# Feed-forward passes of 768 and 1024 tokens with sums kept in PSUM banks, in a fused attention and two-layer feed-forward kernel

## The chip, the cores and the metric

The kernel runs on one core of one Trainium2 chip. The metric is the device time of one execution in microseconds (us); lower is better. The engines are named as in the profile: PE is TensorE (matrix products; PEld is its weight load), DVE is VectorE, ACT is ScalarE, POOL is GpSimd, and SP is the engine whose queue issues nearly all DMA transfers.

## The reference

```python
def _attn_ref(q, k, v, cap):            # 4 batches, 12 heads, 448 tokens, 64 wide
    scores = np.matmul(q, k.transpose(0, 1, 3, 2)) / np.sqrt(q.shape[-1])
    scores = cap * np.tanh(scores / cap)
    attn = np.exp(scores - np.max(scores, axis=-1, keepdims=True))
    attn = attn / (np.sum(attn, axis=-1, keepdims=True) + 1e-09)
    return np.matmul(attn, v)
x = attention, as 1792 tokens x 768
h = x @ w_in;   x = (h - np.tanh(h)) @ w_out               # 768 -> 2048 -> 768
h = x @ w_in2;  out = (h / (1 + np.exp(-1.702 * h))) @ w_out2
```

The four weight matrices arrive as 64-bit floats. All of the feed-forward products are made from two parts of each operand, a high and a low one, so a product of two tiles is three matmuls: high by high, high by low, low by high.

## The kernel before

**Passes.** Attention runs first over 24 pairs of heads (four batches of six). The feed-forward then takes the 1792 tokens in two passes of 896 (two batches each). Each pass has four stages: `gemm_in(0)` (768 to 2048, then h - tanh h, made by `g_cubic` as a chain over ACT and DVE), the way out (2048 to 768), the second way in with its gate, and the rows stage `gemm_rows_seven` (2048 to 768, output rows). The trace's first pass spends 200.1 to 661.4 us in them, the second 661.4 to the end.

**Plain and seven-product stages.** `gemm_in(0)` of both passes, and the way out and the second way in of the first pass (`gemm_out`, `gemm_in(1)`), are plain: every weight chunk against all 896 tokens, in two column spans of 512 and 384 (`SPANS`). The second pass's `gemm_out_seven` and `gemm_in_seven` and both row stages split each operand into 2x2 blocks and make seven block products instead of eight. Operand sums are made on DVE, of the weights ahead of time (`sums_a`, `sums_i`, `sums_b`, through DRAM) and of the activations in the stage (`right`, `left`). Product sums are added on DVE after each product. In the first two of these stages a block is 448 tokens. In the row stage the tokens are the stationary operand in tiles of 128, of which 896 holds seven: six go through the seven products, three to a half, and the seventh by plain products (`rest_products`, with its own split `rest_g`) that need four further weight chunks in each pass.

**Weights.** In the first pass each 64-bit chunk is fetched by DMA (`dbl_dma`, 768 KB, tiles `wd`), converted by ACT and DVE (`conv_exp` L168, `conv_low` L175, `conv_shift` L181, `conv_or` L185 into `wr`) and stored for later (`single`, 384 KB). `conv_or` ends with the store and with the fetch of the chunk three places ahead, whose buffer it has freed. If the chunk is used now, it is split (`wh` on ACT, `wl` on DVE L88). Sixteen chunks of the last matrix are converted beside others (`beside`): twelve in the way out, four in the second way in. So the way out carries 28 conversions and the second way in 20, less what is done early. Chunks are made ready two ahead of use (`LEAD`), in three `wh` buffers.

**Order.** DVE, ACT and SP each run one fixed list, written by the program's order and a scheduler when the kernel is built; a wait in it holds all that stands behind. `late` holds work that is issued some matmuls into the next product. Rows of `left(..)` for the next product stand behind the matmuls that last read the ring of split operands.

Of the kernel before, what the change touches and what calls it, by code (L numbers as in the profile page):

```python
# [37 lines left out]
def attention_moe_moe(ctx, tc, q, k, v, cap, w_in1, w_out1, w_in2, w_out2, out):  # L38
# [60 lines left out]
    xd = [[dr_p.tile([P, S], F32, name=f"xd{b}_{i}") for i in range(KM)] for b in range(B)]  # L99
    wrow = [dr_p.tile([4, NP // 2, S], F32, name=f"wrow{b}") for b in range(B)]  # L100
# [121 lines left out]
    SEVEN_B = ("11", "21", "22", "t2", "t3", "t1", "t4")  # L222
# [9 lines left out]
    for p, m in enumerate(SEVEN_B):  # L232
        rows_stream += [(t, WC, HW) for t in side_b[m]]
        if 2 <= p < 2 + KQ:
            rows_stream.append((side_b["12"][p - 2], WC, HW))
# [125 lines left out]
    def sums_b():  # L361
        for n in range(KH):
            j, a = n // 2, slice(n % 2 * HW, (n % 2 + 1) * HW)
            r = {m: s2[n % 2 * 4 + x][:, :HW] for x, m in enumerate(("11", "21", "12", "22"))}
# [21 lines left out]
    tt, tl, sc_t, ts_t, r_t, sum_t, xs = {}, {}, {}, {}, {}, {}, {}  # L386

# [122 lines left out]
    def pair_out(g):  # L510
        x = xs[g] = xs_p.tile([P, S], F32, tag="xs", name="xs")
        hi_dve(x, r_t.pop(g)[:, :S])
        if g >= NB * NP:
            b, i = divmod(g, NP)
            nc.sync.dma_start(out=xd[b][i], in_=xs.pop(g))
# [7 lines left out]
    def batch_recip(b, half):  # L523
        a = slice(half * S // 2, (half + 1) * S // 2)
        w = w_t[b]
        ins = pin(nc.vector.reciprocal(out=w[:, a], in_=w[:, a]))
        if half:
            for n in range(4):
                nc.sync.dma_start(out=wrow[b][n], in_=w[n * SR:n * SR + NP // 2])
        return ins  # L530

    def w_rows(t, b, i):
        for j in range(2):
            nc.sync.dma_start(out=t[j * D:(j + 1) * D], in_=wrow[b][i % 2 * 2 + j, i // 2].partition_broadcast(D))

    def x_split(s, i, x):
        a = slice(s * S, (s + 1) * S)
        hi_act(xh[i][:, a], x)
        lo_dve(xl[i][:, a], x, xh[i][:, a])
# [4 lines left out]
    def attention():  # L544
# [5 lines left out]
        def x_part(n):  # L550
            s_, i = divmod(n, NP)
            return i, slice(s_ * S, (s_ + 1) * S)
# [21 lines left out]
        for g in range(NG):  # L574
# [3 lines left out]
            for n in x_of(g):  # L578
                pin(nc.vector.tensor_tensor(out=xs[n], in0=xs[n], in1=wb.pop(n), op=ALU.mult))
                i, a = x_part(n)  # L580
                hi_pool(xh[i][:, a], xs[n])
# [15 lines left out]
            for n in x_of(g):  # L597
                i, a = x_part(n)
                lo_pool(xl[i][:, a], xs.pop(n), xh[i][:, a])
# [14 lines left out]
            for n in x_of(g + 1):  # L614
                wb[n] = wb_p.tile([P, S], F32, tag="wb", name="wb")
                w_rows(wb[n], *divmod(n, NP))
# [30 lines left out]
    def swap_pools(**kinds):  # L647
        if "stack" in some:
            some.pop("stack").close()
# [26 lines left out]
    def g_cubic(a, f, ps):  # L676
# [6 lines left out]
        def rest():  # L683
# [19 lines left out]
            if plain[0] and f < KH and a.stop == NT:  # L703
# [7 lines left out]
        if f == KF - 1 and a.stop == NT and not plain[0]:  # L711
            late.append(lambda: list(splits.pop(0)))

    def g_gate(a, f, ps):
# [3 lines left out]
        if plain[0]:  # L718
            g = gr[f][:, a]
            nc.vector.scalar_tensor_tensor(out=g, in0=t, scalar=1.0, in1=ps, op0=ALU.add, op1=ALU.mult)  # L720
            if a.start == 0 and f < KH:
                late.append(lambda: left("11", f))
            if a.stop == NT:
                late.append(lambda: split(rest_g[f], gr[f][:, REST]))
# [6 lines left out]
    TH = 3 * P  # L731
    REST = slice(2 * TH, NT)
    gr, s2, ring, rest_g, last_t = [], [], [], [], []

    def open_plain():
        g_stack.close()
        p = pool("g_plain", 1)
        gr.extend(p.tile([P, NT], F32, name=f"gr{i}") for i in range(KF))
        s2.extend(p.tile([P, S], F32, name=f"gs{i}") for i in range(KH))
        ring.extend([p.tile([P, S], F32R, name=f"r{m}{i}") for m in "hl"] for i in range(KH))  # L740
        rest_g.extend([p.tile([P, P], F32R, name=f"rest{m}{i}") for m in "hl"] for i in range(KF))
# [5 lines left out]

    def right(p, k):
        g11, g12, g21, g22 = (gr[f][:, t * S:(t + 1) * S] for f in (k, KH + k) for t in range(2))
        if p == 1:  # L750
            x = s2[k]
            nc.vector.tensor_tensor(out=x, in0=g22, in1=g12, op=ALU.subtract)
            nc.vector.tensor_tensor(out=x, in0=x, in1=g11, op=ALU.add)
        elif p == 3:
            x = g12
            nc.vector.tensor_tensor(out=g11, in0=g12, in1=g11, op=ALU.subtract)
            nc.vector.tensor_tensor(out=x, in0=g22, in1=x, op=ALU.subtract)
        elif p == 6:
            x = s2[k]
            nc.vector.tensor_tensor(out=x, in0=g21, in1=x, op=ALU.subtract)  # L760
        else:
            x = {0: g11, 2: g21, 4: g11, 5: g22}[p]
        split(ring[k], x)

    def left(name, k):
        g11, g21, g12, g22 = (gr[f][:, t * TH:(t + 1) * TH] for f in (k, KH + k) for t in range(2))
        x = {"11": g11, "21": g12, "22": g12, "t2": s2[k][:, :TH], "t3": g11, "t1": g21, "t4": g22}[name]
        if name == "22":
            s = s2[k][:, :TH]
            add(s, g21, ALU.add, g22)  # L770
            add(s, s, ALU.subtract, g11)
            add(x, x, ALU.subtract, s)
        elif name == "t3":
            add(x, x, ALU.subtract, g21)
        elif name == "t1":
            add(x, x, ALU.add, g22)
        split([t[:, :TH] for t in ring[k]], x)

    def gemm_in(layer):
        for f in range(KF):  # L780
            i, (wh, wl) = w_next()
            for a0, a1 in SPANS:
# [400 lines left out]
```

## Time and profile before

| what | value |
|---|---|
| three runs | 1093.85, 1097.28, 1097.44 us (median 1097.28) |
| profiled execution | 1094.2 us from its first to its last instruction; no other time is given for it |
| PE busy | 1081.3 us (99%), 5579 matmuls |
| DVE busy | 929.8 us (85%) |
| ACT busy | 668.7 us (61%) |
| DMA | 220.58 MB, mean 202 GB/s |
| PE clock granted | 0.9 or more of full speed in all 40 slices |

Busy time of PE is the union of rows whose ends are modelled, and neighbouring matmuls overlap in it; what a matmul costs in a stream is read from the distance of two starts. The kernel has stages with different limits, so the shares of the whole say little about one of them.

### The profile page before, as it was taken

Reading aid. Unit: us, or ns where it says so; the run is one execution under the profiler, and the core shown is the slowest. Engines: PE = TensorE matmul, PEld = TensorE weight load, DVE = VectorE, ACT = ScalarE, POOL = GpSimd, SP = SyncE. Lnnn points to the kernel's source line nnn. Section 1 sums busy time; section 2 is a strip of 40 time slices with the busy share of each in tenths; the row PEclk is TensorE's granted clock in tenths of the full one; section 3 lists DMA queues with packets and bytes.
Section 4 is the critical chain, followed back from the end, with each engine's and each line's share of the span. In section 5 each row is a group of like instructions: output and inputs, shape, how many; then the busy total and the mean of one; then the engine's idle time right before and its main releaser. Section 6 shows DMA issues by size and latency. Waiting matters only on the chain.

```text
span 1094.2 us, 16108 instructions
## 1 busy us (share of the span) xinstructions
PE 1081.3 (99%) x5579; PEld 887.0 (81%) x5579; DVE 929.8 (85%) x1467; ACT 668.7 (61%) x1022; POOL 59.1 (5%) x56
## 2 busy tenths in 40 slices
PE   9999998999999999999999999999999999999998
PEld 3333333688998888899899998889999999999998
DVE  4688999799997787889897885999999898889775
ACT  6898888799893433445245654767645554455453
POOL 0013443200000000000000000000000000000000
PEclk9999999999999999999999999999999999999999
DMA  6767786465537989889835768888555333333344
GB/s 142 206 187 199 192 234 192 148 209 173 188 116 265 318 305 332 292 287 313 285 110 170 227 201 276 313 287 291 183 192 176 107 123 102 102 110 107 119 144 142
DMA packets 156466, 220.58 MB, mean 202 GB/s; under 512 B 58672, under 2 KB 108640, under 8 KB 156384
## 3 DMA queue, kind: packets, MB, share of 16 engines
q1 hardware_dynamic: 155088, 218.94, 62.9%
q8 instruction: 44, 0.72, 0.3%
q10 hardware_dynamic: 1296, 0.61, 0.2%
q14 instruction: 38, 0.31, 0.1%
HBM read 160.83 MB, written 58.68 MB: 201 GB/s over the span
## 4 chain that ended last, share of the span: by engine, by line
PE 85%; DMA 6%; DVE 5%; ACT 2%; issue 2%; SPq 1%; ACTq 0%; DVEq 0%
PE ps_h L791 32%; PE ps_o L1018 15%; PE ps_h L938 10%; PE ps_y L854 10%; PE ps_pv L498 7%; PE ps_sc L457 5%; DMA wd<-in_moe_w_out_dram 4%; PE ps_o L997 3%; DVE wr L185 1%; DVE wd L175 1%; PE ps_qk L436 1%; PE ps_r L505 1%; PE ps_tl L467 1%; PE ps_y L816 1%; ACT wr L168 1%
## 5 line engine op out<-in xcount | busy, mean ns | idle before, releaser
L791 PE MATMUL ps_h<-xh,wh 128*128 128x384 f32 (+1 forms) x576 | 184.5, 365 | 0.3 <-ACT xh L76 0.3
L791 PE MATMUL ps_h<-xl,wh 128*128 128x384 f32 (+1 forms) x576 | 183.8, 364 | 0.0
L791 PE MATMUL ps_h<-xh,wl 128*128 128x384 f32 (+1 forms) x576 | 131.4, 362 | 0.1
L76 ACT CAST rh<-gr 128x384 fp32r<-128x384 f32 (+1 forms) x141 | 73.7, 528 | 82.8 <-PE ps_o L1018 36.4
L791 PEld LDWEIGHTS ps_h<-xh,wh 128*128 128x128 f32 x576 | 107.1, 188 | 13.8 <-ACT xh L76 1.0
L791 PEld LDWEIGHTS ps_h<-xl,wh 128*128 128x128 f32 x576 | 107.0, 188 | 11.9
L76 ACT CAST wh<-whole 128x768 fp32r<-128x768 f32 (+1 forms) x105 | 84.9, 810 | 50.4 <-PE ps_h L938 30.9
L791 PEld LDWEIGHTS ps_h<-xh,wl 128*128 128x128 f32 x576 | 104.6, 188 | 13.4 <-issue 1.4
L1018 PE MATMUL ps_o<-wl,rh 128*128 128x384 f32 x336 | 112.4, 335 | 1.1 <-DVE wl L88 1.1
L1018 PE MATMUL ps_o<-wh,rh 128*128 128x384 f32 x336 | 112.3, 334 | 0.0
L1018 PE MATMUL ps_o<-wh,rl 128*128 128x384 f32 x336 | 112.3, 334 | 0.0
L88 DVE TENSOR_TENSOR wl<-whole,wh 128x768 fp32r<-128x768 f32 (+1 forms) x105 | 96.5, 921 | 9.4 <-ACT wh L76 7.8
L168 ACT ACTIVATE wr<-wd 128x768 f32<-128x768 f32 x64 | 57.9, 909 | 69.6 <-DMA wd<-in_moe_w_out_dram 41.2
L88 DVE TENSOR_TENSOR rl<-gr,rh 128x384 fp32r<-128x384 f32 (+1 forms) x141 | 79.8, 573 | 13.7 <-ACT rh L76 12.9
L476 ACT ACTIVATE t<-ps_sc,tsc 128x896 f32<-128x896 f32 x72 | 70.0, 1008 | 26.6 <-PE ps_sc L457 26.6
L175 DVE TENSOR_SCALAR wd<-wd 128x768 uint16<-128x768 uint16 x57 | 59.5, 1044 | 24.9 <-ACT wr L168 24.7
L478 ACT ACTIVATE t<-t,cpos 128x896 f32<-128x896 f32 x72 | 72.5, 1044 | 0.4
L816 PE MATMUL ps_y<-gh,wh 128*128 128x512 f32 (+1 forms) x192 | 70.0, 365 | 1.6 <-DVE xl L88 1.4
L816 PE MATMUL ps_y<-gl,wh 128*128 128x512 f32 (+1 forms) x192 | 69.9, 364 | 0.0
L457 PE MATMUL ps_sc<-qk 64*128 64x448 f32 x288 | 68.2, 572 | 0.8 <-ACT qk L76 0.6
L498 PE MATMUL ps_pv<-t,rv 128*64 128x448 f32 x288 | 64.2, 551 | 3.9 <-ACT t L476 3.4
L1018 PEld LDWEIGHTS ps_o<-wl,rh 128*128 128x128 f32 x336 | 63.1, 188 | 1.6 <-DVE wl L88 1.4
(145 smaller groups left out, 2307.6 us busy)
## 6 DMA issues: line engine op xcount, KB each, us to landing
wd<-in_moe_w_in_dram SPq DMA_DIRECT2D x64, 384.0 KB
wd<-in_moe_w_out_dram SPq DMA_DIRECT2D x32, 768.0 KB
single<-wr SPq DMA_DIRECT2D x48, 384.0 KB
whole<-single SPq DMA_DIRECT2D x43, 384.0 KB
pair<-single SPq DMA_DIRECT2D x40, 384.0 KB
s<-pair SPq DMA_DIRECT2D x32, 384.0 KB
whole<-s SPq DMA_DIRECT2D x32, 384.0 KB
wh<-kept SPq DMA_DIRECT2D x25, 384.0 KB
```

Of the source, the lines that this page charges most:

```text
L76: pin(nc.scalar.copy(out=dst, in_=src))
L88: pin(nc.vector.tensor_tensor(out=dst, in0=src, in1=hi.bitcast(F32), op=ALU.subtract))
L175: pin(nc.vector.tensor_scalar(out=half[:, :, 2], in0=half[:, :, 1], scalar1=F64_LOW, scalar2=None, op0=ALU.mult))
L457: pin(nc.tensor.matmul(ps[:, j, :S], qk[a, kc], qk[a, :S], start=True, stop=True))
L476: pin(nc.scalar.activation(out=t, in_=ps[:, :, :S], func=AF.Tanh, scale=tsc))
L478: ins = pin(nc.scalar.activation(out=tt[g, c], in_=tt[g, c], func=AF.Exp, scale=cpos))
L498: pin(nc.tensor.matmul(ps[a, :S], w, t[:, j], start=(c == 0), stop=(c == KC - 1)))
L791: pin(nc.tensor.matmul(ps, w[:, kk, :], x[kk][:, a], start=(m == 0), stop=(m == len(seq) - 1)))
L816: nc.tensor.matmul(bank[e][:, :a1 - a0], w[:, kk, c], x[2 * j + kk][:, a0:a1], start=(j == 0 and m == 0), stop=(j == KF // 2 - 1 and m == ...
L854: nc.tensor.matmul(ps[e], w[:, kk, c], x, start=(k == 0 and m == 0), stop=(k == KH - 1 and m == 2))
L938: nc.tensor.matmul(ps, w, x, start=(m == 0), stop=(m == len(seq) - 1))
L1018: nc.tensor.matmul(ps[n], x[:, t], w[:, kk, :], start=(k == 0 and m == 0), stop=(k == KH - 1 and m == 2),)
```

## The change

The token passes become 768 and 1024. Both spans of a plain stage are then equal: 384 and 384 columns in the first pass, 512 and 512 in the second. The halves of the seven-product stages are 384 tokens (rows of pass one) and 512 (all of pass two), so no tile of tokens is left over; `rest_products`, `rest_g` and the four further weight chunks of each pass go away. Batch 1 of the attention output is cut at token 320: its first part is scaled and split during attention as before, the other 128 columns go through DRAM (`parts_of`, `xd`) with batches 2 and 3.

In the seven-product stages the products run in another order, and a later product adds onto the PSUM bank of an earlier one (`head`: for example s3 and 22 onto s2's bank in `gemm_in_seven`). The earlier value is read from the bank between the two. DVE's adds after products go from 7 to 5 for each of the eight steps of `gemm_in_seven`. The activation sums are made in place, four for each `k` of the eight instead of five, and the tiles `s2` are gone.

Two buffers change. The third `wr` buffer is held only through the way out of pass one (`open_plain` closes it); before, it stayed through the second way in too. `sums_b` works in two tiles `more` in the place of `s2`.

```diff
-    NB = 2
-    NPASS = B // NB
+    TOKENS = (6 * P, B * S - 6 * P)
+    FIRST = (0, TOKENS[0])
+    CUT = TOKENS[0] - S
...
-    NT = NB * S
-    SPANS = [(0, 512), (512, NT)]
-    TC = max(z - a for a, z in SPANS)
+    NT = max(TOKENS)
+    SPANS = [[(0, n // 2), (n // 2, n)] for n in TOKENS]
+    HT = NT // 2
+    TC = HT
...
-    SEVEN_B = ("11", "21", "22", "t2", "t3", "t1", "t4")
+    SEVEN_B = ("11", "t2", "21", "t3", "t1", "t4", "22")
...
     def open_plain():
         g_stack.close()
+        some.pop("wr")
+        some.pop("last").close()
         p = pool("g_plain", 1)
         gr.extend(p.tile([P, NT], F32, name=f"gr{i}") for i in range(KF))
...
+    def left(p, k):
+        th = TOKENS[now[0]] // 2
+        g11, g21, g12, g22 = (gr[f][:, t * th:(t + 1) * th] for f in (k, KH + k) for t in range(2))
+        if p == 1:
+            add(g21, g21, ALU.add, g22)
+            sub(g11, g21, g11)
+        elif p == 3:
+            sub(g11, g22, g11)
+        split([t[:, :th] for t in ring[k]], {0: g11, 1: g11, 2: g12, 3: g11, 4: g21, 5: g22, 6: g12}[p])
+        if p == 2:
+            sub(g12, g12, g11)
...
+            for name in ("11", "s2", "s1", "s3", "12", "s4", "22"):
...
+                head = {"12": "11", "s4": "s1", "s3": "s2", "22": "s2"}.get(name, name)
+                if name == head:
+                    banks[head] = ps_next("ps_h")
+                ps = banks[head]
...
+                elif name == "s2":
+                    u2 = temp("q")
+                    add(u2, ps, ALU.add, p1)
+                elif name == "s3":
+                    u3 = temp("t")
+                    add(u3, ps, ALU.add, p1)
+                    add(u3, banks["s1"], ALU.add, u3)
+                    gate(KH + j, HI, u3)
```

Two places on DVE matter below. The first is the end of `gemm_in(0)` of pass one. There `g_far`, `g_t`, `g_q` and `gl` are the steps of h - tanh h of one half of a chunk (the last two chunks here), and `wd`, `wr` and `wl` are the conversion of weight chunks of the next stage. Before:

```order
L698 COPY_PREDICATED g_q<-g_m,g_far 128x512
L88 TENSOR_TENSOR wl<-wr,wh 128x768
L695 TENSOR_TENSOR g_t<-g_v,g_t 128x384
L88 TENSOR_TENSOR gl_2114<-g_q,gh_2098 128x512
L697 SCALAR_TENSOR_TENSOR g_q<-g_q,g_t 128x384
L181 TENSOR_SCALAR wr<-wr 128x768
L698 COPY_PREDICATED g_q<-g_m,g_far 128x384
L185 SCALAR_TENSOR_TENSOR wr<-wd,wr 128x768
L88 TENSOR_TENSOR gl_2114<-g_q,gh_2098 128x384
L175 TENSOR_SCALAR wd<-wd 128x768
L181 TENSOR_SCALAR wr<-wr 128x768
L185 SCALAR_TENSOR_TENSOR wr<-wd,wr 128x768
```

And in the changed kernel:

```order
L183 TENSOR_SCALAR wr<-wr 128x768
L711 TENSOR_TENSOR g_t<-g_v,g_t 128x384
L187 SCALAR_TENSOR_TENSOR wr<-wd,wr 128x768
L90 TENSOR_TENSOR gl_2104<-g_q,gh_2088 128x384
L713 SCALAR_TENSOR_TENSOR g_q<-g_q,g_t 128x384
L177 TENSOR_SCALAR wd<-wd 128x768
L90 TENSOR_TENSOR wl<-wr,wh 128x768
L714 COPY_PREDICATED g_q<-g_m,g_far 128x384
L183 TENSOR_SCALAR wr<-wr 128x768
L187 SCALAR_TENSOR_TENSOR wr<-wd,wr 128x768
L90 TENSOR_TENSOR gl_2104<-g_q,gh_2088 128x384
L177 TENSOR_SCALAR wd<-wd 128x768
```

The steps of h - tanh h all work on 384 columns now, and two conversion steps `wr<-wd,wr` stand ahead of the last `gl` where before one did, the next having stood behind it.

The second place is one step of `gemm_in_seven` in pass two, where `part<-ps_h,part` reads a product's bank, `gr<-gr,..` is the end of a gate, and `gs` is an early operand sum of the row stage. Before:

```order
L907 SCALAR_TENSOR_TENSOR gr_4261<-gr_4261,part 128x448
L88 TENSOR_TENSOR wl<-whole,wh 128x384
L907 SCALAR_TENSOR_TENSOR gr_4254<-gr_4254,part 128x448
L313 TENSOR_TENSOR part<-ps_h,part 128x448
L313 TENSOR_TENSOR gs_4269<-gr_4253,gr_4261 128x384
L313 TENSOR_TENSOR gs_4269<-gs_4269,gr_4253 128x384
L313 TENSOR_TENSOR part<-ps_h,part 128x448
L88 TENSOR_TENSOR wl<-whole,wh 128x768
```

And in the changed kernel, where the second of the three reads here is that of s3's bank and the third that of s1's:

```order
L313 TENSOR_TENSOR part<-ps_h,part 128x512
L921 SCALAR_TENSOR_TENSOR gr_4251<-gr_4251,part 128x512
L313 TENSOR_TENSOR part<-ps_h,part 128x512
L90 TENSOR_TENSOR wl<-whole,wh 128x384
L313 TENSOR_TENSOR part<-ps_h,part 128x512
L90 TENSOR_TENSOR wl<-whole,wh 128x768
L921 SCALAR_TENSOR_TENSOR gr_4252<-gr_4252,part 128x512
L921 SCALAR_TENSOR_TENSOR gr_4244<-gr_4244,ps_h 128x512
```

A weight split stands between the read of s3 and the read of s1, and s1's bank is the one that s4 adds onto one product later.

## Rows read from the trace of the kernel before

**Rows 1.** Busy time by stage: length, engines (instructions), clock, DMA share, GB/s.

```profile
200.10:320.20 120.10, 120.10 (x598) 105.21 (x597) 110.09 (x183) 109.27 (x177) 0.00 (x0) 1.00 0.50 169
320.20:438.70 118.50, 116.93 (x577) 104.18 (x577) 94.54 (x128) 47.90 (x66) 0.00 (x0) 1.00 0.86 295
438.70:555.90 117.20, 116.93 (x578) 104.41 (x578) 100.96 (x173) 48.35 (x88) 0.00 (x0) 1.00 0.83 276
555.90:661.40 105.50, 104.40 (x602) 103.96 (x601) 86.99 (x151) 56.37 (x101) 0.00 (x0) 1.00 0.62 188
661.40:778.10 116.70, 116.61 (x578) 104.35 (x577) 104.63 (x181) 79.16 (x135) 0.00 (x0) 1.00 0.84 292
778.10:882.20 104.10, 104.10 (x505) 94.56 (x505) 98.95 (x168) 55.85 (x99) 0.00 (x0) 1.00 0.46 148
882.20:986.40 104.20, 104.20 (x506) 94.65 (x505) 89.85 (x159) 54.69 (x98) 0.00 (x0) 1.00 0.37 111
986.40:1094.30 107.90, 104.00 (x600) 103.67 (x599) 80.37 (x139) 51.96 (x88) 0.00 (x0) 1.00 0.43 129
```

**Rows 2.** Chain that ended last, in order of time: start, length, what.

```profile
207.81 112.57 PE ps_h L791 x559
...
332.46 5.48 DMA wd<-in_moe_w_out_dram
...
437.65 0.96 DVE wl L88
...
555.94 3.12 PE ps_o L1018 x18
```

**Rows 3.** TensorE timeline, one chunk of the second pass: start, length, instruction.

```profile
690.71 0.39 PE L791 MATMUL ps_h<-xh,wh 128*128 128x512 f32 x1
...
693.47 1.52 PE L791 MATMUL ps_h<-xh,wl 128*128 128x512 f32 x6
...
694.83 0.33 PE L791 MATMUL ps_h<-xh,wh 128*128 128x384 f32 x1
```

**Rows 4.** VectorE groups by shape, first layer of pass one: count, busy, mean ns.

```profile
L698 DVE COPY_PREDICATED g_q<-g_m,g_far 128x512 f32<-128x512 uint16 x15 | 11.2, 745 | 0.3
...
L697 DVE SCALAR_TENSOR_TENSOR g_q<-g_q,g_t 128x512 f32<-128x512 f32 x15 | 10.3, 687 | 1.2 <-ACT g_q L693 0.7
...
L698 DVE COPY_PREDICATED g_q<-g_m,g_far 128x384 f32<-128x384 uint16 x14 | 8.4, 601 | 0.1
...
L697 DVE SCALAR_TENSOR_TENSOR g_q<-g_q,g_t 128x384 f32<-128x384 f32 x14 | 7.9, 563 | 0.3
```

**Rows 5.** Busy time around the second stage, columns as in group 1.

```profile
326.00:332.00 6.00, 6.00 (x31) 5.26 (x30) 6.00 (x12) 2.86 (x6) 0.00 (x0) 1.00 0.01 4
...
338.00:350.00 12.00, 12.00 (x63) 10.96 (x62) 8.03 (x10) 4.07 (x5) 0.00 (x0) 1.00 0.97 351
...
338.00:440.00 102.00, 100.22 (x495) 89.03 (x493) 79.89 (x103) 39.34 (x51) 0.00 (x0) 1.00 0.93 321
```

**Rows 6.** VectorE timeline, the last activation half and the next conversion.

```profile
331.89 0.55 DVE L88 TENSOR_TENSOR gl<-g_q,gh 128x384 fp32r<-128x384 f32 x1
...
333.99 0.96 DVE L185 SCALAR_TENSOR_TENSOR wr<-wd,wr 128x768 uint32<-128x768 uint32 x1
```

**Rows 7.** Conversion step L185, two stretches: count, durations, first and last start.

```profile
L185 DVE SCALAR_TENSOR_TENSOR wr<-wd,wr x28: 936/958/961, 334.0 to 436.8; 128x768 uint32<-128x768 uint32 x28
...
L185 DVE SCALAR_TENSOR_TENSOR wr<-wd,wr x16: 948/959/975, 441.5 to 530.2; 128x768 uint32<-128x768 uint32 x16
```

**Rows 8.** Who waited for whom in the second stage: us, times, longest.

```profile
ACT wr L168 <- DMA wd<-in_moe_w_out_dram: 34.0, 15, 4.3
```

**Rows 9.** VectorE groups by shape, row stage of pass one.

```profile
L88 DVE TENSOR_TENSOR rl<-gr,rh 128x384 fp32r<-128x384 f32 x40 | 21.6, 550 | 1.5 <-ACT rh L76 1.4
...
L88 DVE TENSOR_TENSOR wl<-whole,wh 128x768 fp32r<-128x768 f32 x21 | 19.8, 950 | 2.1 <-ACT wh L76 2.1
```

**Rows 10.** Who waited for whom, ACT, second way in: us, times, longest.

```profile
ACT wr L168 <- DVE wl L88: 4.4, 7, 1.0
```

More of the change, by code (lines that the diff above doesn't have):

```diff
@@ L647, in swap_pools @@
     def swap_pools(**kinds):
-        if "stack" in some:
-            some.pop("stack").close()
+        for name in ("last", "stack"):
+            if name in some:
+                some.pop(name).close()
         some.clear()
@@ L710, in g_cubic @@
         late.append(rest_behind)
-        if f == KF - 1 and a.stop == NT and not plain[0]:
+        if f == KF - 1 and a.start and not plain[0]:
             late.append(lambda: list(splits.pop(0)))
@@ L971, in gemm_rows_seven @@
[L971 to L973 removed]
+            got, banks = {}, {}
+            p1 = u2 = u3 = None
+            for name in ("11", "s2", "s1", "s3", "12", "s4", "22"):
+                c, n = chunk_of[name], half_of.get(name, 0)
+                if j == 0:
+                    c, n = {"12": 3}.get(name, c), {"12": 0, "22": 1}.get(name, n)
+                first = c not in got
+                if first:
+                    got[c] = w_next()
+                i, (wh, wl) = got[c]
+                head = {"12": "11", "s4": "s1", "s3": "s2", "22": "s2"}.get(name, name)
+                if name == head:
+                    banks[head] = ps_next("ps_h")
+                ps = banks[head]
+                seq = [
+                    (w[:, 3 * n + kk, :], x[:, :HT]) for kk, (h, l) in enumerate(right_of[name])
+                    for w, x in ((wh, h), (wh, l), (wl, h))
+                ]
+                for m, (w, x) in enumerate(seq):
+                    nc.tensor.matmul(
+                        ps, w, x, start=(name == head and m == 0),
+                        stop=(m == len(seq) - 1), skip_group_check=True,
+                    )
+                    if m == 0 and first:
+                        ahead(i)
+                    if m == 3:
+                        run_late()
+                if name == "11":
+                    p1 = temp("far")
+                    nc.scalar.copy(out=p1, in_=ps)
+                elif name == "s2":
[6 more added lines that the diff above has]
+                    gate(KH + j, HI, u3)
+                elif name == "12":
+                    gate(j, LO, ps)
+                elif name == "s4":
+                    add(u2, ps, ALU.add, u2)
+                    gate(j, HI, u2)
+                elif name == "22":
+                    add(p1, ps, ALU.add, p1)
+                    gate(KH + j, LO, p1)
+                if j == KH - 1 and name in ("12", "s4", "22"):
+                    a = {"12": 0, "s4": 3, "22": 6}[name]
+                    late.extend(lambda k=k: left(0, k) for k in range(a, min(a + 3, KH)))
@@ L983, in gemm_rows_seven @@
-        third.append(sums[3])
-        rest = [ps_s.tile([P, 512], F32, tag="s", name="ps_o")[:, :HW] for _ in range(2)]
-        todo = [divmod(n, KM) for n in range(2 * KM)] if b0 + NB < B else []
+        room = [t[:, a:a + HW] for t in (*four_of_pairs(), more[0]) for a in range(0, t.shape[1], HW)]
+        p1, u2, u3 = (room[m * nt:(m + 1) * nt] for m in range(3))
+        third.append(more[1][:, :WC])
+        todo = [divmod(n, KM) for n in range(2 * KM)] if another else []
         loaded = []
@@ L992, in add_to @@
             nc.vector.scalar_tensor_tensor(out=dst, in0=ps, scalar=0.5, in1=x, op0=ALU.mult, op1=ALU.add)
-        def rest_products(k, f, half, wh, wl, first, last):
-            gh_f, gl_f = rest_g[f]
-            for m, (x, w) in enumerate(((gh_f, wh), (gh_f, wl), (gl_f, wh))):
-                nc.tensor.matmul(
-                    rest[half], x, w, start=(first and k == 0 and m == 0), stop=(last and k == KH - 1 and m == 2)
-                )
-        last = []
-        for p, name in enumerate(SEVEN_B):
-            ps = three()
-            end = p == 6 and b0 + NB == B
+        last, of = [], {}
+        if side:
+            until("b")
+        for p, name in enumerate(SEVEN_B):
+            head = {"21": "11", "t3": "t2", "t4": "t2", "22": "t1"}.get(name, name)
+            if name == head:
+                of[head] = banks()
+            ps = of[head]
+            end = p == 6 and not another
             for j in range(KQ):
@@ L1012, in gemm_rows_seven @@
                 last.clear()
-                order = [(n, *k) for n in range(3) for k in ks] if end else [(n, *k) for k in ks for n in range(3)]
+                order = [(n, *k) for n in range(nt) for k in ks] if end else [(n, *k) for k in ks for n in range(nt)]
                 for n, k, kk, u, v in order:
```

323 lines of the change are left out of this document (127 added, 196 removed).

## The prediction

> **What bounds the kernel now.** I read the stages first, then the chain, then the starts of matmuls, and last what DVE, ACT and the DMA do where the chain leaves PE. By stage [rows 1] PE is busy nearly throughout, but its cover differs: in the first layer of pass one DVE has 110.1 of 120.1 us; in the way out and the second way in the DMA share is 0.86 and 0.83; in pass two DVE is high (99.0 of 104.1 on the way out) and the DMA has room. The chain [rows 2] says the same. It runs along PE through the first layer (559 matmuls in 112.57 us), leaves PE early in the way out, goes through weight transfers and conversion steps from 332.46 to a weight split at 437.65 us, and runs along PE again, with 18 row matmuls in 3.12 us. So in the way out conversions arrive barely in time, and everywhere else matmuls set the time.
>
> A conversion there waits for its transfer: ACT's first step waited 34.0 us in 15 waits for weights [rows 8]. From 338 to 440 us the DMA engines are 0.93 busy at 321 GB/s; their best stretch has 0.97 and 351 [rows 5]. The reader is to see that this stage has two bounds within a few per cent of each other, and that only one of them depends on the number of tokens: weights are the same for 768 tokens as for 896.
>
> **What matmuls alone give.** By the distance of starts a 512-column matmul costs (694.83 - 690.71) / 18 = 228.9 ns, the last six of a span 226.7 [rows 3]. The first layer's mean is 112.57 / 559 = 201.4 ns, so its 384-column ones cost 173.9; in the rows they cost 3.12 / 18 = 173.3 [rows 2].
>
> Pass one: the first layer saves 559 x (201.4 - 173.9) ns = 15.4 us; the two further plain stages of 576 matmuls take 100.2 us each instead of 118.5 and 117.2 [rows 1], which saves 18.3 and 17.0; the rows have 504 matmuls for 600, 87.4 us instead of 105.5, which saves 18.1. Together -68.8. Pass two: 576 x 228.9 = 131.8 us instead of 116.7 (+15.1); twice 504 x 228.9 = 115.4 instead of 104.1 and 104.2 (+22.5); the rows 672 x 173.3 = 116.5 instead of 104.0 (+12.5). Together +50.1. So PE alone would be 18.7 us shorter. The tail behind the last matmul (107.9 - 104.0 = 3.9 us) stays.
>
> No trace here shows a stage of 512 columns only; I take 228.9, with 226.7 as the lower bound: 1584 x 2.2 ns = 3.5 us. The Trainium skill ("TensorE: Matmul & The Clock Gate", Back-to-back issue gap) gives N / 2.4 + 2.5 ns for an isolated gap, about 216 ns at 512 columns. By it the second pass would be some 20 us shorter than in my sum; the rows at 512, and those at 384 (173.3 against some 162), stand above the rule.
>
> **What the conversions take back.** The first layer of pass one leaves DVE behind. Its last activation step ends at 332.4 us, 12 us after PE has left the stage, and the next conversion step starts at 334.0 [rows 6]; from 326 to 332 the DMA stands still [rows 5], since the fetches stand behind these steps. In the change DVE's five steps per half are done on 384 columns instead of 512 in one half of two: 745 - 601 = 144 ns for the dearest, 687 - 563 = 124 for the cheapest [rows 4]. Five of these are 0.62 to 0.72 us a chunk, 16 chunks about 10.6 us. A conversion step that stood behind the last step now stands ahead of it (first place in the order shown), some 1.5 us more. So conversions resume 12 us earlier, not the 15.4 that PE gains.
>
> From there the work is unchanged: 28 conversions from 334.0 to 436.8, 3.81 us apart, and 16 more from 441.5 to 530.2 [rows 7]. None waits for more tokens, so a faster PE pulls none forward. At 12 us earlier the last is done at 519; the DMA may close ranks in the second way in, where its share is lower, and I take 4 us for that. Then come the last chunk's split and 36 matmuls of 173.9 ns: 515 + 2.5 + 6.3 = 524 us. PE alone would be there at 555.9 - 15.4 - 18.3 - 17.0 = 505. **The term is +19 us.** Bounds: at 351 GB/s throughout, the 195 us from 332 to 527 at about 321 become 178, and the stage ends near 510 (+5); with a shift of 9 us and no closing up it ends at 531 (+26). I take 524, since the shares of 0.93 leave little to close. The Trainium skill ("DMA: Bandwidth & Descriptors", Where 436 GB/s comes from) puts the HBM side at about 358 GB/s for one core; the best stretch's 351 agrees. By 358 throughout the stage would end near 507; this page speaks against a gain beyond that.
>
> The third `wr` buffer is missing in the second way in. With three, ACT waited 4.4 us for a split to free one [rows 10]. With two, this may double (4.4) or hide in the transfers (0); I take 2.
>
> **The rows of pass one.** DVE is busy 87.0 of 105.5 us [rows 1]. Ring splits (0.550 us) and weight splits (0.950) [rows 9] become few less: 28 weight chunks instead of 32, 15 bank reads instead of 24, the scaling of x 14% more. That leaves about 81 us under 87.4 of PE, 92% where it was 83%. The stage lost 1.5 us then; I add 2.6 now, with 0 and 8 as bounds.
>
> **Shared banks in pass two.** In `gemm_in_seven` a product is 9 matmuls, 2.06 us. Between s3's end and s4's first matmul DVE must read s3's bank, make a weight split and read s1's bank (second place in the order): 0.687 [rows 4] + 0.950 + 0.687 = 2.3 us. Eight steps lose 0.27 us each, 2.2 us; I take 2. Below, nothing, where the split is the half one; above, if each split also waits for its copy on ACT about as long as it lasts itself, 8 x 1.2 = 10. On the way out each bank has two thirds of a short round, 12 matmuls or 2.7 us, before it is written again, and DVE has less to do per matmul than before: nothing.
>
> Costed at nothing: the additional small transfers of batch 1 during attention (DMA off its path there), the operand sums of the rows, four for five (DVE, inside the 92%), `gemm_in(0)` of pass two, whose DMA share of 0.84 now has 15 us more room.
>
> **Sum.** -18.7 + 19 + 2 + 2.6 + 2 = +6.9 us on the profiled 1094.2, so 1101.1. That execution is 3.1 us under the median of the runs; the same step on 1097.3 gives **1104**.
>
> **Rivals.**
> (A) As above, 1104, from 1094 to 1113 by the bounds of the conversions: 0.51.
> (B) The other side: conversions follow PE. Their pace was then set by the three `wh` buffers that PE frees, and a faster PE brings it along. For it: the second way in has a DMA share of only 0.83, and PE hardly waits there. Against it: 34 us of ACT waits for transfers [rows 8], and the chain through them. The +19 shrinks; it decides below +7, and at 0 gives 1085: 0.14.
> (C) Splits wait in pass two as well, and shared banks cost 10 instead of 2, in `gemm_in_seven`: 1112. For it, DVE's fixed list; against, its 89.9 of 104.2 us there [rows 1]: 0.13.
> (D) Pass one loses more than the cover: two `wr` buffers at 4.4, no closing up (+4), rows bound by DVE at 95 us (+5): 1115. For it, 92%; against, three terms on their upper side: 0.17.
> (E) The 512-column stream runs better alone than mixed: 226.7 ns everywhere, 3.5 us less, 1100. The Trainium skill's gap (the page named above) would make it 1084. No stretch of rows shows less than 226.7: 0.05.
>
> The measurement tells about 0.5%, 5.5 us, from no change: 1091.8 to 1102.8. Faster: B nearly whole and the low edge of A, 0.17. Same: a third of A, most of E and some of B, 0.28. Slower: the rest of A, C and D, 0.55. The range takes in B's near side and D: 1087 to 1119; likeliest alone, 1094 to 1113.
>
> **What would show it.** Right: the first layer of pass one near 105 us; the way out and second way in well above 100 us each, together near 219 from 305 to 524; weight waits on PE there; row stage near 90; pass two at 132, 115, 117 and 120. Wrong: plain stages of pass one near 100 us (then B), 512-column starts off 229 ns, waits of PE for DVE reads in `gemm_in_seven` above 0.5 us a step, or a DMA share far under 0.9 in the way out while PE waits.

## The result

The changed kernel takes **1110.71 us** (median of 4 runs, 1108.82 to 1112.10) against 1095.73 (4 runs, 1093.85 to 1097.44) for the kernel before beside it. The ratio is 1.0144, with a 95% interval of 1.0119 to 1.0168: slower by about 15 us. Its profiled execution spans 1110.2 us; the device time is some 1.9 us above the span in each of these runs.

**The profile after.** First the busy time by stage, which answers to [rows 1] and has attention as its first row (length; PE, PEld, DVE, ACT, POOL busy with instructions; granted clock, DMA share, GB/s):

```profile
0.00:195.80 195.80, 191.06 (x1047) 70.97 (x1047) 159.95 (x193) 165.18 (x177) 56.52 (x56) 1.00 0.70 196
195.80:299.50 103.70, 103.70 (x598) 100.81 (x597) 95.51 (x176) 97.31 (x172) 0.00 (x0) 1.00 0.55 184
299.50:411.80 112.30, 105.16 (x578) 100.61 (x576) 90.27 (x126) 48.23 (x70) 0.00 (x0) 0.98 0.84 291
411.80:524.50 112.70, 104.17 (x576) 102.89 (x577) 100.20 (x159) 48.36 (x77) 0.00 (x0) 0.97 0.89 300
524.50:627.70 103.20, 94.99 (x506) 92.88 (x505) 80.33 (x137) 52.63 (x94) 0.00 (x0) 0.93 0.70 210
627.70:758.30 130.60, 130.60 (x578) 108.15 (x577) 116.87 (x183) 83.88 (x133) 0.00 (x0) 1.00 0.79 271
758.30:872.60 114.30, 114.30 (x506) 94.62 (x506) 99.38 (x152) 63.40 (x104) 0.00 (x0) 1.00 0.38 117
872.60:989.80 117.20, 116.11 (x506) 93.83 (x505) 84.38 (x127) 52.76 (x84) 0.00 (x0) 1.00 0.32 94
989.80:1110.20 120.40, 116.64 (x673) 116.32 (x671) 82.75 (x123) 53.93 (x85) 0.00 (x0) 1.00 0.37 107
```

The reader is to see two passes of a different kind. Pass two is PE from end to end: 482.5 us, 49.6 more than before, as matmuls alone say. Pass one was to lose 68.8 us and lost 29.4 (461.3 to 431.9): in its last three stages PE stands still for 7 to 9 us each (length less busy), and the granted clock is under 1, which it was in no stage of before.

The chain of work that ended last (start, length, what) answers to [rows 2]:

```profile
202.56 44.09 PE ps_h L800 x253
...
324.02 7.08 DMA wd<-in_moe_w_out_dram
...
533.17 6.35 DMA w<-wrow
541.22 35.23 PE ps_o L1035 x187
...
590.59 4.78 DMA whole<-t
597.27 4.46 PE ps_o L1035 x15
...
627.91 130.60 PE ps_h L800 x576
```

Before, it left PE on the way out and returned with the second way in. Now it leaves PE in the first layer already, at 246.65 us (202.56 + 44.09), and stays away longer: it goes through transfers (`w<-wrow`, `whole<-t`) in the row stage too.

On the way out, the same chain close up shows one round of a weight chunk:

```profile
324.02 7.08 DMA wd<-in_moe_w_out_dram
331.18 0.90 ACT wr L170
332.11 1.05 DVE wd L177
333.57 0.97 DVE wr L187
334.62 0.84 ACT wh L78
337.82 0.97 DVE wr L187
338.81 0.34 SPq L191
339.24 7.84 DMA wd<-in_moe_w_out_dram
```

A fetch lands, ACT and DVE convert it and the next one, and only the end of a conversion lets SP store the result and issue the next fetch into that buffer. From one such fetch to the next on the chain pass 15.22 us, and four conversions lie between (the fetches that follow them were issued at 326.35, 330.59, 334.99 and 339.24): 3.81 us a chunk, what it was in [rows 7].

### The profile page after: what moved, and what is told of

Its sections match the earlier page's. It is cut to its first block, busy times and chain, and to the rows that moved or that the text cites. A ratio compares the mean times of both kernels' runs of the same rounds, so it can differ in the third digit from the quotient of the medians.

```text
span 1110.2 us, 15923 instructions
## 1 busy us (share of the span) xinstructions
PE 1076.7 (97%) x5555; PEld 881.1 (79%) x5555; DVE 909.6 (82%) x1368; ACT 665.7 (60%) x989; POOL 56.5 (5%) x56
## 2 busy tenths in 40 slices
DMA packets 156201, 218.22 MB, mean 197 GB/s; under 512 B 58652, under 2 KB 106328, under 8 KB 156120
## 4 chain that ended last, share of the span: by engine, by line
PE 69%; DVE 12%; DMA 10%; ACT 4%; issue 3%; SPq 1%; DVEq 0%; ACTq 0%
PE ps_h L800 17%; PE ps_o L1035 16%; PE ps_y L869 10%; PE ps_h L960 10%; PE ps_pv L507 7%; PE ps_sc L466 5%; DMA wd<-in_moe_w_out_dram 3%; DVE wd L177 3%; DMA wd<-in_moe_w_in_dram 3%; DVE wr L187 2%; ACT wh L78 1%; DVE wl L90 1%; DMA w<-wrow 1%; DVE wr L183 1%; PE ps_qk L445 1%
## 5 line engine op out<-in xcount | busy, mean ns | idle before, releaser
L800 PE MATMUL ps_h<-xl,wh 128*128 128x384 f32 (+1 forms) x576 | 177.3, 353 | 0.0
L78 ACT CAST rh<-gr 128x512 fp32r<-128x512 f32 (+1 forms) x173 | 100.3, 585 | 119.9 <-PE ps_o L1035 66.4
L90 DVE TENSOR_TENSOR rl<-gr,rh 128x512 fp32r<-128x512 f32 (+1 forms) x173 | 110.0, 644 | 42.3 <-ACT rh L78 40.1
L1035 PE MATMUL ps_o<-wh,rh 128*128 128x384 f32 x392 | 132.8, 340 | 7.2 <-ACT wh L78 7.2
L1035 PE MATMUL ps_o<-wl,rh 128*128 128x384 f32 x392 | 134.1, 342 | 1.0 <-DVE wl L90 1.0
L1035 PE MATMUL ps_o<-wh,rl 128*128 128x384 f32 x392 | 133.5, 341 | 0.0
L1035 PEld LDWEIGHTS ps_o<-wh,rh 128*128 128x128 f32 x392 | 75.0, 192 | 8.2 <-ACT wh L78 8.2
L170 ACT ACTIVATE wr<-wd 128x768 f32<-128x768 f32 x64 | 58.1, 910 | 35.9 <-DMA wd<-in_moe_w_out_dram 25.1
L1035 PEld LDWEIGHTS ps_o<-wl,rh 128*128 128x128 f32 x392 | 75.6, 193 | 2.2 <-DVE wl L90 2.0
L1035 PEld LDWEIGHTS ps_o<-wh,rl 128*128 128x128 f32 x392 | 75.6, 193 | 0.0
L825 PE MATMUL ps_y<-gh,wh 128*128 128x384 f32 x192 | 65.4, 341 | 5.5 <-ACT wh L78 5.4
```

What stands on the lines that cost most here:

```text
L78: pin(nc.scalar.copy(out=dst, in_=src))
L90: pin(nc.vector.tensor_tensor(out=dst, in0=src, in1=hi.bitcast(F32), op=ALU.subtract))
L800: pin(nc.tensor.matmul(ps, w[:, kk, :], x[kk][:, a], start=(m == 0), stop=(m == len(seq) - 1)))
L825: nc.tensor.matmul(bank[e][:, :a1 - a0], w[:, kk, c], x[2 * j + kk][:, a0:a1], start=(j == 0 and m == 0), stop=(j == KF // 2 - 1 and m == ...
L1035: nc.tensor.matmul(ps[n], x[:, t], w[:, kk, :], start=(name == head and k == 0 and m == 0), stop=(k == KH - 1 and m == 2), skip_group_chec ...
```

## The experiments

All change the kernel after, but for e4, e8 and e12, which change the one before. Stage lengths are the distances of the first matmuls of neighbouring stages on PE. A ratio is to the kernel before, run beside it (medians 1093.57 to 1095.73), with its 95% interval; where none stands, the time is of one run.

| run | way out | second way in | rows, pass one | us | ratio |
|---|---|---|---|---|---|
| before | 118.5 | 117.2 | 105.5 | 1095.73 | |
| after | 112.3 | 112.7 | 103.2 | 1110.71 | 1.0144 (1.0119 to 1.0168) |
| e1 half of the x loads | 109.3 | 113.6 | 92.5 | 1099.28 | 1.0046 (1.0027 to 1.0065) |
| e2 their loads on POOL | 108.7 | 114.3 | 98.7 | 1106.35 | 1.0114 (1.0084 to 1.0144) |
| e3 no weight sums | 107.7 | 100.3 | 91.1 | 1082.63 | |
| e4 before, no weight sums | 120.0 | 116.3 | 105.4 | 1094.5 | |
| e5 sums moved, not added | 111.2 | 109.0 | 97.4 | 1101.66 | |
| e6 one conversion step less | 103.3 | 105.3 | 101.4 | 1092.7 | |
| e7 third wr buffer | 110.0 | 111.8 | 103.4 | 1109.35 | 1.0139 (1.0121 to 1.0158) |
| e9 fourth fetch buffer | 105.4 | 116.6 | 101.8 | 1105.63 | 1.0095 (1.0062 to 1.0128) |
| e10 that step on ACT | 112.6 | 114.2 | 100.6 | 1110.22 | 1.0146 (1.0121 to 1.0171) |
| e11 e2, e9, e10 together | 105.8 | 119.9 | 93.4 | 1103.45 | 1.0091 (1.0061 to 1.0121) |

Two further runs on the kernel before: e8 (shared banks) 1094.7, 1.0010 (0.9995 to 1.0025), and e12 (the step on ACT) 1096.86, 1.0021 (1.0005 to 1.0037).

A stage length is that of one profiled execution, and it scatters. On the way out, DVE, ACT and SP run the same lists in the kernel after, e1, e2, e3, e5 and e7, since their edits lie in later stages; the stage took 112.3, 109.3, 108.7, 107.7, 111.2 and 110.0 us. So a difference of less than some 5 us there says little, and the kernel after is the longest of the six. In the second way in, e1 and e2 have the lists of the kernel after but for one or two places: 112.7 to 114.3 us. In the rows, e10 has: 103.2 and 100.6. Where an edit does bear on a stage, the scheduler has written the rest of that stage's lists in another order too, e9 and e10 on the way out excepted, so a difference there is that of the edit and the new order together.

**What holds the rows of pass one (e1, e2).** PE's timeline in that stage shows the longest wait, what comes after it, and a later wait:

```profile
536.66 0.33 PE L1035 MATMUL ps_o<-wl,rh 128*128 128x384 f32 x1
536.83 0.34 PE L1035 MATMUL ps_o<-wh,rl 128*128 128x384 f32 x1
539.93 0.69 PE L1035 MATMUL ps_o<-wh,rh 128*128 128x384 f32 x1 [2.77 <-ACT wh L78]
541.22 0.69 PE L1035 MATMUL ps_o<-wl,rh 128*128 128x384 f32 x1 [0.59 <-DVE wl L90]
541.70 0.52 PE L1035 MATMUL ps_o<-wh,rl 128*128 128x384 f32 x1
542.02 0.52 PE L1035 MATMUL ps_o<-wh,rh 128*128 128x384 f32 x1
...
596.28 0.79 PE L1035 MATMUL ps_o<-wh,rh 128*128 128x384 f32 x3 [2.41 <-ACT wh L78]
```

At the first place weights are late by 2.77 and 0.59 us, the high part first and then the low one. ACT's and DVE's timelines at the same place say what they waited for:

```profile
539.05 0.83 ACT L78 CAST wh<-more 128x768 fp32r<-128x768 f32 x1 [4.63 <-DMA more<-t]
539.60 0.69 DVE L1098 TENSOR_TENSOR x<-x,w 128x512 f32<-128x512 f32 x1 [4.58 <-DMA w<-wrow]
540.21 0.95 DVE L90 TENSOR_TENSOR wl<-more,wh 128x768 fp32r<-128x768 f32 x1
```

The 2.77 us are ACT's: it stood 4.63 us for a weight sum that comes back through DRAM (`more<-t`). DVE stood 4.58 us before a scaling of x, which nobody needs until pass two, because its factors `w<-wrow` had not come, and the low part of the split is the next in its list. But that part needs the high one, which was done at 539.88, so DVE's stand cost 0.3 us here. At the later wait, 2.41 us up to 596.28, the loads of x do count, as the chain through it shows:

```profile
587.47 0.10 DVE x L1098
589.02 0.70 DVE xl L90
589.73 0.33 SPq L1092
595.39 0.84 ACT wh L78
```

The factors `w<-wrow`, issued at 582.17, come at 587.33; x is scaled and split, which frees its buffer, and only then does SP issue the next load of x (L1092) and, behind it, the weight fetch `whole<-t` (590.59). The first edit leaves out six of the twelve loads and scalings of x, with their transfers, so part of pass two computes on other data:

```diff
-        todo = [divmod(n, KM) for n in range(2 * KM)] if another else []
+        todo = [(1, i) for i in range(KM)] if another else []
```

> The changed kernel with six of the twelve loads and scalings of x for pass two left out of the row stage of pass one (the first half of the tokens keeps stale columns). Theory 1 (weight chunks stand behind these loads and scalings in SP's and DVE's lists; PE waits for them and then runs some microseconds at its lower clock): the row stage falls from 103.2 us to 92 to 97, the whole by 6 to 11 us to about 1101. Rival (the stage is held by the weights' own transfers and the split work on DVE, 92 per cent): within 3 us of 1110.7.

The stage fell to 92.5, as theory 1 had it: PE's waits from 8.2 to 3.3 us, and its busy time from 95.0 to 89.2 as the clock rose from 0.93 to 0.98. The wait for the weight sum stayed (2.48 us). The second edit keeps all the work and moves these loads (x, and `w` likewise) past SP's queue:

```diff
-        nc.sync.dma_start(out=x, in_=xd[i][:, a])
+        nc.gpsimd.dma_start(out=x, in_=xd[i][:, a])
```

> The changed kernel with the same twelve loads of x and its weights issued on GpSimd's queue, where nothing else is issued in that stage, in place of SP's. Theory 1: a load that waits for its tile no longer holds a weight chunk, the row stage falls to 90 to 95 us and the whole to about 1100. Rival (DVE's list holds the scaling ahead of a weight split, whatever queue the load is on): the stage stays at 100 or more, the whole within 4 us of 1110.7; if issuing from GpSimd makes the loads land later, it gets longer.

98.7 us and 1106.35, between theory and rival: less than half of what e1 gave. PE still waited 7.2 us, 4.8 of them in one wait for the same weight sum, for which ACT waited:

```profile
ACT wh L78 <- DMA more<-t: 4.6, 1, 4.6
```

So SP's queue is part of it, and the late weight sum, which neither edit touches, is another. How e1's fall divides into transfers, DVE's work and places in the lists is not shown, since it takes away all three.

**What the weight sums cost (e3, e4, e5).** `sums_b` prepares operand sums of the last matrix in pass one: 218.22 - 205.62 = 12.6 MB of transfers and 32 additions, no word of which stands in the prediction. The edit leaves the sums out and lets the row products read plain quarters; e4 is the same on the kernel before. Both are single runs.

```diff
-            side.append(sums_b())
+            done.add("b")
```

> The changed kernel without the operand sums of the last weight matrix (the four summed quarters are replaced by plain quarters), so without 12.6 MB of transfers and 32 additions on DVE in the second way in of pass one. Theory 1 (conversions and transfers pace that stage): it falls from 112.7 us to 100 to 104, and with no chunk of sums late at the start of the rows that stage falls too; the whole falls by 10 to 18 us to 1092 to 1100. Rival (the fixed lists, not transfers, make the waits): the stage stays above 108 and the whole falls by under 5 us.

> The kernel before without the same operand sums. Theory 1 (with 896 tokens PE covers conversions and transfers in this stage): the second way in stays at 116 to 117 us, the whole within 4 us of 1095.7. Rival (transfers cost before as well): it falls by 8 us or more.

e4 moved no stage of pass one by more than 1.5 us; e3 is the largest fall of all, some 10 us beyond its forecast. The second way in, in windows of e3:

```profile
407.40:507.70 100.30, 100.22 (x576) 99.90 (x577) 86.75 (x132) 47.34 (x77) 0.00 (x0) 1.00 0.73 241
```

PE's 100.2 us are the whole stage. Under 896 tokens the sums lay in the shade of matmuls. Under 768 the whole is 28 us longer with them (1110.71 - 1082.63): 12.4 in the second way in and 12.1 in the rows, 24.5 together, and 4.6 on the way out, whose lists are the same, which is scatter. With the sums out of both kernels the change is 12 us faster (1082.63 and 1094.5); with them in it is 15 us slower. In e5 the sums' transfers stay and their additions are left out (the sums are wrong values):

```diff
-            add(r["22"], r["22"], ALU.subtract, r["12"])
...
+            yield
```

> The changed kernel with all transfers of the operand sums of the last matrix, but without the 32 additions between load and store. Tells transfers from DVE's additions in the 28 us that leaving out both took away. If the transfers pace the second way in (theory 1), it stays at 108 to 113 us and the whole is 1102 to 1111. If the additions in DVE's fixed list pace it, it falls to 100 to 104 and the whole to 1085 to 1095.

Of the 12.4 us of the second way in, 3.7 go with the additions; 8.7 stay with the transfers and their places in SP's list. Among SP's waits in that stage of the kernel after (us, times, longest), a store of a sum is held for its addition, with the weight fetches behind it:

```profile
SPq L376 <- DVE more L313: 31.0, 25, 5.4
```

In e5 a store is held for its load instead, 10.5 us in 8 waits. So the long hold of 31.0 us was worth 3.7 us at most; whether bytes or places in the list make the other 8.7 was not told apart.

**What paces the way out (e6, e9, e10).** My word was transfers. e6 leaves one conversion step (`conv_low`, 1.04 us on DVE) out of the 48 later chunks; weights then lack their low bits:

```diff
-            pin(nc.vector.tensor_scalar(
-                out=half[:, :, 2], in0=half[:, :, 1], scalar1=F64_LOW, scalar2=None, op0=ALU.mult
-            ))
+            return
```

> The changed kernel without the step that makes the low bits of the 48 later weight chunks on DVE (1.04 us each, 28 of them in the way out). Theory 1 (the way out is paced by transfers): it stays within 3 us of 112.3, the whole falls by under 5 us. Rival (it is paced by the conversion steps on DVE and ACT one behind another): it falls by 6 us or more towards the 100 us of its matmuls, the whole by 8 to 20.

The way out fell to 103.3 us, 4.4 below the shortest of the six, and nearly the same bytes came at 310 GB/s in the place of 291, so the transfers had not been at their limit. That is the rival's outcome, in one run, and with DVE's list of the stage in a new order. The kernel after shows the same in its second way in: 12 us at more than the 351 and 358 GB/s by which the prediction bounded the transfers.

```profile
455.00:467.00 12.00, 10.00 (x58) 9.68 (x56) 11.20 (x19) 5.53 (x9) 0.00 (x0) 1.00 1.06 381
```

e9 leaves all work in and adds a fourth fetch buffer up to the end of the way out:

```diff
-            more = some.get("wd") if n_dbl[0] % 3 == 0 else None
+            wd2 = some.get("wd2")
+            if wd2:
+                more = (some["wd"], wd2, None, None)[n_dbl[0] % 4]
+            else:
+                more = some.get("wd") if n_dbl[0] % 3 == 0 else None
...
+                                some["wd2"] = some["last"].enter_context(tc.tile_pool(name="some_wd2", bufs=1, side="right"))
+                                dbl_dma()
```

> The changed kernel with a fourth buffer for 64-bit weight chunks in the way out of pass one, kept up to the end of that stage; nothing is left out. Theory 1 (what paces the way out is the round of one chunk through its buffer: transfer, ACT step, DVE steps, and only then the next fetch): a fourth buffer lets the next fetch start a conversion earlier; the way out falls from 112 to 103 to 108 us, the second way in is unchanged near 112, the whole 1101 to 1107. Rival (the DMA engines set the pace by themselves): way out 110 to 113, whole 1108 to 1112. Rival (DVE's list sets the pace, with its 95.5 us of work in 112 and its waits for ACT): the fetch is early and nothing else moves, way out 110 to 113, but ACT's first step waits less than the 25 us for transfers that it waits now.

Its way out and second way in, in windows, and ACT's wait for weights on the way out, in the kernel after and in e9:

```profile
300.00:405.40 105.40, 102.23 (x578) 101.24 (x578) 91.33 (x128) 49.33 (x71) 0.00 (x0) 0.98 0.90 323
405.40:522.00 116.60, 105.88 (x577) 104.92 (x577) 97.44 (x154) 46.60 (x75) 0.00 (x0) 0.94 0.85 278
```

```profile
ACT wr L170 <- DMA wd<-in_moe_w_out_dram: 25.1, 14, 4.3
```

```profile
ACT wr L174 <- DMA wd<-in_moe_w_out_dram: 4.7, 2, 2.9
```

Theory 1 held: with the same DVE work and nearly the same lists the stage took 105.4 us (and 105.8 in e11, which has this buffer too), 2.3 to 6.9 below the six, and ACT's wait, 20.7 to 25.1 us in the six, was nearly gone. But 3.9 us were given back in the second way in, where the buffer is closed again and the sums run; which of the two, or the new order of the lists there, was not shown. The Trainium skill ("Perfetto Trace Analysis", Optimization Strategy) reads a gap that repeats on the engine that should be saturated as a possible lack of SBUF for the next tile; the trace agrees in part: with one more buffer the way out is shorter than any of the six, and PE's waits in it are 3.1 us, where the six have 3.3 to 5.6. e10 moves the step to ACT for 16 chunks and leaves nothing out:

```diff
-        conv_low(i, i < KF)
+        conv_low(i, i < KF or i >= R0)
```

> The changed kernel with one conversion step (conv_low, 1.04 us on DVE) done on ACT for the 16 chunks that are converted beside others, 12 of them in the way out and 4 in the second way in; nothing is left out. Theory 1 (DVE's steps are part of the round that sets the pace): about 0.4 of what leaving the step out altogether gave, so the way out falls from 112 to 107 to 109, the second way in from 112.7 to 108 to 111, the whole 1101 to 1106. Rival (the transfers set the pace, and the kernel without the step gained because its data came with fewer collisions): no stage moves by more than 1.5 us, whole 1108 to 1112. A third outcome: ACT's step lengthens the round as much as DVE's shortens it; then the way out is 112 to 115.

It is the third outcome: on ACT the step takes 1.96 us, DVE now waits for it, and a DVE with 10 us less work on the way out (79.8 for 90.3) is no faster (112.6 us, above the six):

```profile
327.97 1.96 ACT wd L175
```

```profile
DVE wr L187 <- ACT wd L175: 14.7, 11, 1.4
```

So on the way out it is the length of the round, not DVE's busy share, that counts.

**Smaller terms (e7, e8).** e7 keeps the third `wr` buffer through the second way in:

```diff
     def open_plain():
         g_stack.close()
-        some.pop("wr")
-        some.pop("last").close()
```

> The changed kernel with the third wr buffer kept through the second way in, as before the change. The prediction put its loss at 2 us, with 0 and 4.4 as bounds: the whole falls to 1106 to 1110, in the second way in alone. Rival: two buffers were the main cause of that stage's waits; it falls to 104 or less and the whole to 1100 or less.

The stage was 0.9 us shorter, within its scatter, and the whole by no more than two sets of runs can tell. The rival, that two buffers were the main cause of the waits, fell. e8 puts the shared banks and the sums in place into the kernel before, with its halves of 448, in pass two's way out and second way in:

```diff
-            ps = three()
+            head = {"11": "11", "12": "11", "s1": "s1", "s4": "s1"}.get(name, "s2")
+            if name == head:
+                banks[head] = three()
+            ps = banks[head]
```

> The kernel before, tokens in 896 and 896, with only the shared banks and the in-place sums in the two seven-product stages of pass two. With 448 columns a product of 9 matmuls is 1.86 us, shorter than the 2.2 us of two reads and a weight split on DVE: the second way in of pass two gets 1 to 4 us longer, the way out stays at 104, the whole is 1096 to 1100. Rival (fewer additions on DVE help): the whole is under 1094.

The two stages took 104.2 and 104.3 us, as before; neither the expected loss nor the rival's gain came.

**Candidates (e11, e12).** e11 joins e2, e9 and e10; e12 is e10's step on the kernel before.

> The changed kernel with three edits together: the fourth weight buffer, the conversion step on ACT for the 16 chunks, and the loads of the row stage on POOL's queue; nothing is left out. If the three gains add up (each by itself: 3 to 8, 5 to 9, and the 4.4 measured), the whole is 1090 to 1098, about the kernel before. If the first two take the same wait, 1098 to 1103. If neither of the two helps, 1105 to 1108.

> The kernel before with the same conversion step on ACT for the same 16 chunks; nothing is left out. Its matmuls take 100 of the 118.5 us of its way out and of the 117.2 of its second way in, at 896 tokens (116 us of PE work each), so by both theories PE alone is nearly the bound there: the way out can fall by at most 1.6 us of PE's waits and the whole to about 1092. If ACT's step holds its other work up, the way out gets longer: 1096 to 1100. Likeliest: 1092 to 1096, not to be told from no change.

e11 is the best version with all the work in it, at 0.9% over the kernel before, just beyond the middle one of its three cases: its rows take 93.4 us at a full clock, but the second way in took back what the way out gained. e12 stands 0.2% above (interval from 1.0005), no more than the medians of the kernel before differ; its second way in took 120.4 us for 117.2, on the side that its expectation named for ACT holding up other work. (The 100 us of matmuls named there are those of 768 tokens; for 896 it is the 116 behind them.) No version that computes everything beat the kernel before.

## Why the prediction was right, and where not

The forecast was 1104 in a range of 1087 to 1119, slower the likeliest; it came to 1110.7. On profiled spans the sum said 1101.1 and the trace has 1110.2. The difference of 9.1 us, by stage: attention -4.3, the three stages up to the rows +2.8, the rows of pass one +13.2, pass two -2.5. So the direction, and the loss in the two conversion stages, came as forecast; that the whole is this near is in part luck, as attention and pass two made good half of what the rows lost. The rows went beyond their own bounds, and the weight sums, 24.5 us by e3, have no term. Rival A's range does not follow from its own bounds either: +5 and +26 in the place of +19 give 1090 to 1111, not 1094 to 1113.

**Pass two: right.** 130.6, 114.3, 117.2 and 120.4 us stand against 132, 115, 117 and 120. The 512-column matmul takes 130.60 / 576 = 226.7 ns in the chain above, the lower bound and not the 228.9 that was taken. By the isolated gap of about 216 ns (the Trainium skill, "TensorE: Matmul & The Clock Gate", Back-to-back issue gap) the first layer would take 124 us, an estimate; the trace shows 130.6.

**Conversions: size right, cause only partly.** The last step of h - tanh h, which answers to [rows 6]:

```profile
314.82 0.55 DVE L90 TENSOR_TENSOR gl<-g_q,gh 128x384 fp32r<-128x384 f32 x1
```

And the conversions of the second way in, as in [rows 7] (count, durations, first and last start):

```profile
L187 DVE SCALAR_TENSOR_TENSOR wr<-wd,wr x19: 934/958/975, 415.5 to 514.1; 128x768 uint32<-128x768 uint32 x19
```

The activation ends 17.1 us earlier, of which 4.3 are attention's: 12.8 for the 12 forecast. The last conversion is 16.1 us earlier, less 4.3 is 11.8: a faster PE pulled nothing forward, and the 4 us of closing up that I gave did not come. The last 44 conversions took 196 us from the first start to the last in both kernels (334.0 to 530.2, and 318.0 to 514.1). The second way in ended at 524.5 for 524, but that this fits so well is luck, since attention made good what closing up did not. From the start of the first layer, PE alone would take 305 us there; it took 328.7, so 23.7 us were taken back, and 19 and 2 were forecast. Without the weight sums (e3) the same three stages took 311.7, so the conversions by themselves took back some 7 us (11 with the longest way out of the six). The rest came with the sums, which have no term of their own but stood in the pace that [rows 7] gave: the size of the +19 is right, and as the price of conversions it is luck. What failed is that transfers are the pace, and that "the shares of 0.93 leave little to close": on the way out e6 and e9 show a round with three buffers, with room in the transfers (323 GB/s over the stage in e9, and 381 in the row above), and in the second way in e3 shows the sums. Rival B fell nonetheless: the faster PE did not shorten that round.

**The rows of pass one: the mis-sized term.** "I add 2.6 now, with 0 and 8 as bounds" on 87.4 measured 15.8, and rival D's 95 us was also too low. The reasoning went by DVE's busy share, about 81 us under 87.4; DVE's 80.3 us came as said, but in a stage of 103.2, so its work was not the bound. What counts is what comes late at a few places: weight sums through DRAM (e3: 12.1 us less without) and weight fetches behind the loads of x (e1: 10.7 less with half of them). The two overlap, as their sum exceeds the loss. In PE's waits of the stage (us, times, longest)

```profile
PE ps_o L1035 <- ACT wh L78: 7.2, 3, 2.8
PE ps_o L1035 <- DVE wl L90: 1.0, 3, 0.6
```

are 8.2 us; most of the remaining 7.6 is the clock (0.93 over 95 us of busy PE; more below).

**Shared banks: size near, mechanism smaller.** 2.2 us in `gemm_in_seven` were forecast, 0.27 in each of eight steps; it takes 117.2, against 504 x 226.7 ns = 114.3, 2.9 more. PE's waits there show 0.9 us, and only 0.2 are for a read of a bank:

```profile
PE ps_h L960 <- ACT wh L78: 0.7, 1, 0.7
PE ps_h L960 <- DVE part L313: 0.2, 1, 0.2
```

The distances of starts show more. In each of the six middle steps the weight load of s4 waits for DVE's read of s1's bank, and two matmuls start 0.31 us apart in the place of 0.227:

```profile
898.07 0.69 DVE L313 TENSOR_TENSOR part<-ps_h,part 128x512 f32<-128x512 f32 x1
898.80 0.19 PEld L960 LDWEIGHTS ps_h<-xh,wh 128*128 128x128 f32 x1 [0.23 <-DVE part L313]
898.83 0.47 PE L960 MATMUL ps_h<-xh,wh 128*128 128x512 f32 x1
899.14 0.39 PE L960 MATMUL ps_h<-xl,wh 128*128 128x512 f32 x1
```

That is 0.08 us a step, 0.5 in all; the split between the two reads is the half one (0.55 us, as in the order shown), for which the sum took 0.950. Most of the rest lies in the first step (1.0 us for a late weight at 884.41, 0.7 for reads of banks by ACT and DVE) and the last (0.5 for such a read). Rival C's 10 us fell. With 448 tokens the order cost nothing (e8); 512 columns without shared banks were not run. Two `wr` buffers: 0.9 us by e7, for 2, not told from scatter.

**Attention** took 195.8 us for 200.1. Three runs on the kernel before had 197.6 to 198.0 in place of 200.1, so about half of this is that one execution's; what makes the rest shorter was not tried.

## What to carry to other kernels

Work that is the same for any number of tokens (conversions, operand sums, loads for the next pass) is paid for by the matmuls above it. Before taking tokens from the pass that carries it, list all of it, also what never showed in a wait: the sums that cost nothing at 896 tokens cost some 25 us at 768. And where an engine runs one fixed list, a busy share says little: look for what stands ahead of the urgent instruction, for how many buffers a fetch must wait, and, where two engines stand at once, for which of them the waiting one needed first.

## What was not expected of the hardware

After the 2.77 us wait above PE ran at its lower clock. The starts from 541.70 on are 0.32 us apart, where 0.17 is the distance before the wait. In windows of 530 to 536 and 541.5 to 546.5 us the granted clock is:

```profile
530.00:536.00 6.00, 6.00 (x37) 6.00 (x36) 4.73 (x10) 2.33 (x5) 0.00 (x0) 1.00 0.72 224
541.50:546.50 5.00, 5.00 (x16) 5.00 (x16) 4.57 (x8) 2.85 (x6) 0.00 (x0) 0.50 0.78 266
```

Full speed (2.4 GHz) ahead, half (1.2 GHz) behind. These 16 matmuls cost 16 x 0.147 = 2.4 us more than 16 at 173 ns, nearly the wait over again, with PE shown as busy. The same came after the wait that ended at 596.28 us: 15 matmuls in 4.46 us in the chain, 297 ns each. The Trainium skill ("TensorE: Matmul & The Clock Gate", Back-to-back issue gap) gives N / 1.2 ns for the lower clock, 320 ns at 384 columns, and the trace agrees. A weight that comes 2.8 us late thus cost about 5 here, by this estimate, and the prediction priced no wait in this way.
